# A linear-attention block and a multilayer perceptron on one core: a new order for the same instructions

## The chip, the core and the metric

The kernel runs on one core of a Trainium2 chip. The metric is the device time of one execution in microseconds (us); a kernel's time is the median of its runs. A core has a TensorE (matrix products; PE in the profile, its weight loads PEld), a VectorE (DVE), a ScalarE (ACT), a GpSimd (POOL) and a SyncE (SP), which here only issues transfers (DMAs). Each engine works through its own list of instructions in order and waits on semaphores for the others.

## The reference

Four batches of 768 tokens, eight heads of 48 elements. First a gated linear attention, then a block with layer norm and two matrices of 384 x 1536 and 1536 x 384:

```python
for t in range(S):
    state = alpha[:, :, t, :, None] * state + np.einsum('bhd,bhe->bhde', k[:, :, t], v[:, :, t])
    y[:, :, t] = np.einsum('bhd,bhde->bhe', q[:, :, t], state)
...
x = y.transpose(0, 2, 1, 3).reshape(B, S, H * D)
xn = (x - mu) / np.sqrt(var + 1e-06) * g_ln
out = x + np.maximum(xn @ w_ch1, 0.0) @ w_ch2
```

## The kernel before

The tokens are cut into six chunks (c = 0 to 5) of 128, and each chunk is worked on for four batches (b = 0 to 3). All matrix products are in float32, each of two TensorE instructions.

**Attention** (`attention`, L278): 24 generators, one for each chunk and batch. Each loads its inputs, takes the logarithm of the gates (L292), sums it along the tokens with a triangular matrix on TensorE (L298 in chunk 0, L303 later), takes exponentials (L306, L307), scales k and q on DVE (L309, L311), transposes them (L336), copies the transposes out of PSUM (L341, L343), forms the scores (L352 in chunk 0, L360 later), masks them on DVE (L367, L372), forms the update of the state (L388), adds it on DVE (L397, L401) and gates it on POOL (L403), forms the output (L414 in chunk 0, L426 for odd and L429 for even batches later), moves it out (L437 to L443), normalises it (L456 to L470), transposes it (L476) and scales it into xT (L479, L483). From chunk 1 on, the chunk is cut into halves of 64 tokens, so that L303, L360, L388, L426 and L429 are products on 64 or 48 rows that share the TensorE array.

**Weights** (`take_weights`, L229): the two matrices come as twelve pieces of 768 KB in 64-bit floats (six of the first matrix, six of the second), through three buffers `ws`. A piece is loaded (L205) and made 32-bit in three DVE instructions (L217, L219, L221), one on ACT (L223) and two on DVE (L225, L227); then the piece three further on is loaded into its buffer.

**Perceptron.** Chunk 0 uses the plain products: `hidden` (L506, with a ReLU on ACT, L509) and `project` (L518). Chunks 1 to 5 use fast matrix multiplications with fewer products: 15 products of combined blocks (`hidden_product`, L795) in two rounds for the first matrix, and 20 (`product`, L618) for the second. The combined blocks are made on DVE: of the first matrix once (`combine_first`, L744), of the second once (`combine_weights`, L578), of xT for each chunk (`combine_x`, L769), of the hidden values for each chunk (`combine_hidden`, L605). The results of the products are gathered by sums on DVE (L805 to L838, L628, L631) and POOL (L814 to L834, L634), the ReLUs of chunks 1 to 5 are on ACT (L846), and the outputs are sent by SP (L497).

**PSUM.** All TensorE results, of the attention and of the perceptron, share one pool of eight banks (`tag="bank", bufs=8`); an accumulator can be opened when a bank has been read out.

**The order.** Nothing is scheduled by the framework: each piece of work is a Python generator that yields after a few instructions, and the string `ORDER` (L25 to L46) says whose turn is next. The instructions of all engines, DMA issues too, are written down in the order of these turns. In this document turn n is the letter at place n of `ORDER`, counted from 0; there are 1566. The letters:

```python
turns = {"YZ"[h]: first_of_chunk_0(h) for h in range(2)}
turns |= {"PQ"[h]: second_of_chunk_0(h) for h in range(2)}
turns |= {chr(ord("a") + n): attention(n // B, n % B) for n in range(NCB * B)}
turns |= {chr(ord("A") + i): take_weights(i) for i in range(len(pieces))}
turns |= {"M": mlp(), "V": hidden_products(NCB - 1), "S": combine_first(), "W": combine_weights(), "R": relus(),
          "X": (x for c in range(1, NCB) for x in combine_x(c)),
          "N": (x for c in range(1, NCB) for x in combine_hidden(c)), "O": outputs()}
```

So a to x are the attentions, A to L the weight pieces, Y and Z the hidden layer of chunk 0 for batches 0, 1 and 2, 3, P and Q its projection, M the products of chunks 1 to 5 (without the first matrix of chunk 5, which is V), R the ReLUs, S, W, X and N the combinations, and O the loads of x for the output sums. M and V yield twice for each product: the TensorE instructions are one turn (four of L795 or eight of L618), the sums that read the accumulator the next.

Of the kernel before, what the change touches and what calls it, by code (L numbers as in the profile page):

```python
# [22 lines left out]


ORDER = (  # L25
    "acacababcdaacabdbaabdcacabbacbbababceccbaAcfcdbadaacecacfeafdedebdfbeadbaedeecge"
    "adbAacgAfedghbgeedfecfafgfcefdAgeddbbgfdfghffbebaigcjbibffhjBhcdcYhCfcgccehYfedh"
    "cfedeedhgdedYjAfidBfjiBZhjhZZfBYegfhgjhghCiZYBYiCYYhfhghhkggZilihjZjgiZCiDjYDZZZ"
    "ghZYEYjkeiYkiDiEijgljjjlghYCYhiYkhYFEZhiFigYEZigkikDYZZlkkeejlYlgjhFlZlmYkZgknlg"
    "jZSGkHmiknlSljlkiljkjlGiHlmlllZimFhmZYgYmmjZiYhmheeHmGlkfSnZlnZefSQnmfiGHZghkkeo"  # L30
    "IYmSkiISkJgjIjommmOmJPJnSnQgopPghlKPIKhKjiPOnLSnSfSXkmQLffQOLXWkimXPQSWmPPXpnOpW"
    "XmnnXSmXSQomWnnpnmSoXmQMlmlkXkWliMnnMoXXpjWSWSMjMMoMoMlSMnMMWMoMknMMpMMqMMMMMOPi"
    "npnMopMMrmOMjkpMpopopRqoMoirQkplppnqprRppqWMMWMMnMWMqlMRrMMMMkMqRMMMjkrqRMrMMpsk"
    "oMoMMqMMRRnqpMMRjMqMMoWqOqsnRpqlsoqqpMsNtRNpMMNMjNoMoMMMosRqMMMOkNooMqtNMNMMMtMo"
    "MRlNNsmkNMpqMMNtMMMNlMrMMNMMNqMtqMsrMMWNnrrqMMMNMMstnMXvMsMMvXXprXorrXXXrqMMMXXM"
    "MMMMMMMsXqMMOmvMMMMMMMuXMMMMMMmtRMmttMRrtMrMMttrstvMtqussvsqtMMMMqMrMMrvMMMrRMMM"
    "MRMtMnMRMMmssmrMrrpOtsORMuRMoRMsMMMMoRNMMNtMMNMpqMMMoRNMRNMNNMMNRNOMnNMMMrstMpMN"
    "toNMNMMMMMrMnuoOMsMuNMvxMMuMNrpMOMNovMMvMMvMpMMMXtXMxvvMsXvssXXsXtvMXMuMXuXMMMMM"
    "usMMMtwMMMMMMvMMvwuuuRuuXuuuLxvXOMMMMMMMMMMMwMwxMrMuMswMuMMMwMMsvRxRvMMsMMRwMMxM"
    "xMqwMxMMxMwRtMMMxwMMMMxRqruwtxRwxswxxwRxwuxwRMNvNwMRMNrvwNRMMMMMMtNwNNquNNRrsvst"  # L40
    "tMNMJxMOMMMNNMxMMMvMqMuwxxMNtMtMMMMxuwXMwMMNXMXMMNMvNMXXuMXMXMMxXMXwMMXwMMMvMwMM"
    "MxMMMMMMMXMMMMMOuMuMMRMMMMMMMMwMMMMMMMMMRMMvxMMRMRxwMMMROMuMRMvOwxMMRRMwMRxMNMOM"
    "uMvMMXRVNMMMXXMMRMXXXXMMNVNVXVVXMVNMMVVVMVRVNXVVVVVNRVVMNXVVMVRVMVMVNVNMNVVVMVMV"
    "VMRVRVMVVVMVMVONVMVMNMVMMMRVMNNVRVVVVMVVROVMMMVMNVRVVRVMVMVMNMVRKMOMMMRNNMNMMNMM"
    "MMMNVNMNMNVMMMMNRONMMMNMMNMMMNMMMMNMMMNMMMMMMM"
)  # L46


# [860 lines left out]
```

## Time and profile before

| | |
|---|---|
| median of three runs | 434.6 us |
| lowest and highest run | 433.5, 435.28 us |
| span of the profiled execution, first to last instruction | 431.0 us |
| median less this span | 3.6 us |
| mean granted TensorE clock | 0.999 |
| instructions | 11676 |
| moved by DMA | 45.53 MB |

The profile is one execution; its own time isn't given beside its span, so the 3.6 us are the part of a median run that lies around the span. Lines such as L618 are those of the kernel's source; "out<-in" names tiles, without their buffer numbers. "busy" is the time in which an engine ran an instruction, "idle before" the time that it stood still ahead of one, followed by what ended the wait. The chain of waits is followed back from the last instruction, at each step to what released it; its rows have a start, a length, and an engine with tile, line and number of instructions. Ends of matmuls are modelled, and some matmul records are missing, so counts in rows can be low.

### The profile page before, as it was taken

The page shows a single profiled execution, that of the slowest core. Times are in us where ns is not written, and L with a number is a line of the kernel's source. Part 1 is how long each engine was busy: PE and PEld are TensorE (multiplying, and loading weights), DVE is VectorE, ACT ScalarE, POOL GpSimd, SP SyncE. Part 2 cuts the span into 40 slices and gives each one's busy share as a digit, 9 for nine tenths or more (in the row PEclk, how much of TensorE's full clock was granted, in tenths as well). Part 3 has the DMA queues.
Part 4 walks back from the last instruction along what each step waited for, and adds up shares of the span by engine and source line. Part 5 has one row for each costly group of instructions (what it writes and reads, how often), then busy time and mean ns, then how long its engine had stood idle before and what let it go on. Part 6 is the DMA issues. An engine that isn't in the chain of part 4 may idle for free.

```text
span 431.0 us, 11676 instructions
## 1 busy us (share of the span) xinstructions
PE 425.7 (99%) x4760; PEld 378.2 (88%) x4760; DVE 333.2 (77%) x644; ACT 200.0 (46%) x519; POOL 152.7 (35%) x164
## 2 busy tenths in 40 slices
PE   8999999999999999999999999999999999999997
PEld 6788888866588889998889998889998899999996
DVE  4989899999998888866769756757686668948683
ACT  6597466774043882325385134384415562221100
POOL 1011031110205382252563243580153661647423
PEclk9999999999999999999999999999999999999999
DMA  8979968774117354031150141400014000011201
GB/s 287 288 208 272 308 151 257 203 247 142 38 56 212 107 148 141 29 105 45 52 151 23 49 120 38 94 2 22 2 56 146 2 1 2 0 39 37 75 18 55
DMA packets 55517, 45.53 MB, mean 106 GB/s; under 512 B 26748, under 2 KB 51580, under 8 KB 55464
## 3 DMA queue, kind: packets, MB, share of 16 engines
q1 hardware_dynamic: 54920, 44.63, 35.0%
q8 instruction: 37, 0.61, 0.6%
q10 hardware_dynamic: 544, 0.17, 0.2%
q14 instruction: 16, 0.13, 0.1%
HBM read 35.25 MB, written 9.53 MB: 104 GB/s over the span
## 4 chain that ended last, share of the span: by engine, by line
PE 94%; DVE 2%; DMA 1%; ACT 1%; SPq 0%; issue 0%; DVEq 0%
PE hps L795 30%; PE ops L618 30%; PE ops L518 7%; PE hps L506 6%; PE tps L336 4%; PE aps L360 3%; PE ups L388 2%; PE yps L426 2%; PE yps L429 2%; PE xps L476 2%; DMA ws<-in_moe_w_ch_dram 1%; PE lps L303 1%; PE aps L352 1%; PE lps L244 1%; PE lps L298 1%; PE yps L414 1%
## 5 line engine op out<-in xcount | busy, mean ns | idle before, releaser
L795 PE MATMUL hps<-sum,w 128*128 128x256 f32 x192 | 48.0, 381 | 0.0
L634 POOL TENSOR_TENSOR ob<-ob,u 128x192 f32<-128x192 f32 x40 | 27.0, 685 | 58.9 <-DVE ob L631 44.3
L618 PE MATMUL ops<-w,hT 128*128 128x192 f32 x224 | 40.7, 328 | 0.0
L795 PEld LDWEIGHTS hps<-sum,w 128*128 128x128 f32 x192 | 35.7, 190 | 4.7 <-ACT hT L825 0.2
L618 PEld LDWEIGHTS ops<-w,hT 128*128 128x128 f32 x224 | 36.9, 190 | 1.0 <-issue 0.6
L403 POOL TENSOR_TENSOR mid<-mid,gate 112x192 f32<-112x192 f32 x20 | 13.3, 668 | 68.7 <-DVE mid L401 19.7
L795 PE MATMUL hps<-xT,w 128*128 128x256 f32 x136 | 34.4, 380 | 0.0
L506 PE MATMUL hps<-xT,w 128*128 128x256 f32 x144 | 34.0, 384 | 0.1
L846 ACT ACTIVATE hT<-hT 128x512 f32<-128x512 f32 x48 | 28.8, 625 | 10.4 <-POOL hT L817 7.1
L518 PE MATMUL ops<-w,hT 128*128 128x384 f32 x96 | 32.8, 490 | 0.0
L628 DVE TENSOR_TENSOR ob<-ops,ob 128x192 f32<-128x192 f32 x50 | 17.6, 353 | 17.7 <-PE ops L618 9.4
L506 PEld LDWEIGHTS hps<-xT,w 128*128 128x128 f32 x144 | 26.3, 190 | 4.0 <-DVE xT L479 0.6
L618 PE MATMUL ops<-ws,sum 128*128 128x192 f32 x160 | 29.2, 327 | 0.0
L814 POOL TENSOR_TENSOR hT<-hT,u 128x512 f32<-128x512 f32 x8 | 10.4, 1305 | 53.0 <-DVE u L813 53.0
L795 PEld LDWEIGHTS hps<-xT,w 128*128 128x128 f32 x136 | 25.5, 190 | 3.2
L518 PEld LDWEIGHTS ops<-w,hT 128*128 128x128 f32 x96 | 17.6, 190 | 10.5
L618 PEld LDWEIGHTS ops<-ws,sum 128*128 128x128 f32 x160 | 26.4, 190 | 0.2
L336 PE MATMUL tps<-consts,qk 128*112 128x128 f32 x176 | 25.3, 275 | 0.2 <-DVE qk L311 0.2
L336 PEld LDWEIGHTS tps<-consts,qk 128*112 128x112 f32 x176 | 20.3, 134 | 4.3 <-DVE qk L311 0.8
L460 ACT ACTIVATE xn<-x,few 128x384 f32<-128x384 f32 x24 | 14.8, 615 | 18.7 <-DVE few L456 17.5
L618 PE MATMUL ops<-ws,hT 128*128 128x192 f32 x128 | 23.4, 327 | 0.0
L618 PE MATMUL ops<-more,sum 128*128 128x192 f32 x120 | 22.0, 327 | 0.0
(243 smaller groups left out, 1172.9 us busy)
## 6 DMA issues: line engine op xcount, KB each, us to landing
ws<-in_moe_w_ch_dram SPq DMA_DIRECT2D x12, 768.0 KB
vn<-in_v_dram SPq DMA_DIRECT2D x12, 384.0 KB
kept<-x SPq DMA_DIRECT2D x24, 192.0 KB
ob<-kept SPq DMA_DIRECT2D x24, 192.0 KB
out_dram<-ob SPq DMA_DIRECT2D x19, 192.0 KB
ra<-in_alpha_dram SPq DMA_DIRECT2D x14, 192.0 KB
rk<-in_k_dram SPq DMA_DIRECT2D x6, 384.0 KB
rq<-in_q_dram SPq DMA_DIRECT2D x6, 384.0 KB
```

The source lines that it names most:

```text
L336: nc.tensor.transpose(tps[:, p], qk_of(c, b)[:, i, p].rearrange("p a b -> p (a b)")[:, :R], ident)
L360: nc.tensor.matmul(aps[0][halves[i if cross else 1 - i], p, s], kT[rs, p, s], qT[rs, p, s], start=True, stop=True)
L403: nc.gpsimd.tensor_mul(new, new, by)
L460: act(out=xn, in_=x, func=AFT.Square, bias=mean, accum_out=dev)
L506: nc.tensor.matmul(hps, w1[:, j // 2, f, j % 2 * P:][:, :P], xT_of[0][:, f, bs], start=(f == 0), stop=(f == NF - 1))
L518: nc.tensor.matmul(ops_of[b], hT_of[c][:, j, b], w2[:, j], start=(j == 0), stop=(j == NJ - 1))
L618: nc.tensor.matmul(acc, lhs[:, j], rhs[:, j], start=(j == 0), stop=(j == NT - 1))
L628: nc.vector.tensor_add(x, acc, x)
L634: getattr(nc.gpsimd, f"tensor_{op}")(x, x, y)
L795: nc.tensor.matmul(acc[:, i], w, b, start=True, stop=True)
L814: add_late(c4, c4, u2)
L846: nc.scalar.activation(out=x, in_=x, func=AFT.Relu)
```

## The change

Turns 0 to 61 and the last seven stay. All others are put in a new sequence. Each letter occurs as often as before, so every generator issues the same instructions in its own order; the instructions, tiles, buffers and engines are the same, and the order between generators differs, on every engine and on SP.

```diff
 ORDER = (
-    "acacababcdaacabdbaabdcacabbacbbababceccbaAcfcdbadaacecacfeafdedebdfbeadbaedeecge"
-    "adbAacgAfedghbgeedfecfafgfcefdAgeddbbgfdfghffbebaigcjbibffhjBhcdcYhCfcgccehYfedh"
-    "cfedeedhgdedYjAfidBfjiBZhjhZZfBYegfhgjhghCiZYBYiCYYhfhghhkggZilihjZjgiZCiDjYDZZZ"
-    "ghZYEYjkeiYkiDiEijgljjjlghYCYhiYkhYFEZhiFigYEZigkikDYZZlkkeejlYlgjhFlZlmYkZgknlg"
-    "jZSGkHmiknlSljlkiljkjlGiHlmlllZimFhmZYgYmmjZiYhmheeHmGlkfSnZlnZefSQnmfiGHZghkkeo"
-    "IYmSkiISkJgjIjommmOmJPJnSnQgopPghlKPIKhKjiPOnLSnSfSXkmQLffQOLXWkimXPQSWmPPXpnOpW"
-    "XmnnXSmXSQomWnnpnmSoXmQMlmlkXkWliMnnMoXXpjWSWSMjMMoMoMlSMnMMWMoMknMMpMMqMMMMMOPi"
-    "npnMopMMrmOMjkpMpopopRqoMoirQkplppnqprRppqWMMWMMnMWMqlMRrMMMMkMqRMMMjkrqRMrMMpsk"
-    "oMoMMqMMRRnqpMMRjMqMMoWqOqsnRpqlsoqqpMsNtRNpMMNMjNoMoMMMosRqMMMOkNooMqtNMNMMMtMo"
-    "MRlNNsmkNMpqMMNtMMMNlMrMMNMMNqMtqMsrMMWNnrrqMMMNMMstnMXvMsMMvXXprXorrXXXrqMMMXXM"
-    "MMMMMMMsXqMMOmvMMMMMMMuXMMMMMMmtRMmttMRrtMrMMttrstvMtqussvsqtMMMMqMrMMrvMMMrRMMM"
-    "MRMtMnMRMMmssmrMrrpOtsORMuRMoRMsMMMMoRNMMNtMMNMpqMMMoRNMRNMNNMMNRNOMnNMMMrstMpMN"
-    "toNMNMMMMMrMnuoOMsMuNMvxMMuMNrpMOMNovMMvMMvMpMMMXtXMxvvMsXvssXXsXtvMXMuMXuXMMMMM"
-    "usMMMtwMMMMMMvMMvwuuuRuuXuuuLxvXOMMMMMMMMMMMwMwxMrMuMswMuMMMwMMsvRxRvMMsMMRwMMxM"
-    "xMqwMxMMxMwRtMMMxwMMMMxRqruwtxRwxswxxwRxwuxwRMNvNwMRMNrvwNRMMMMMMtNwNNquNNRrsvst"
-    "tMNMJxMOMMMNNMxMMMvMqMuwxxMNtMtMMMMxuwXMwMMNXMXMMNMvNMXXuMXMXMMxXMXwMMXwMMMvMwMM"
-    "MxMMMMMMMXMMMMMOuMuMMRMMMMMMMMwMMMMMMMMMRMMvxMMRMRxwMMMROMuMRMvOwxMMRRMwMRxMNMOM"
-    "uMvMMXRVNMMMXXMMRMXXXXMMNVNVXVVXMVNMMVVVMVRVNXVVVVVNRVVMNXVVMVRVMVMVNVNMNVVVMVMV"
-    "VMRVRVMVVVMVMVONVMVMNMVMMMRVMNNVRVVVVMVVROVMMMVMNVRVVRVMVMVMNMVRKMOMMMRNNMNMMNMM"
-    "MMMNVNMNMNVMMMMNRONMMMNMMNMMMNMMMMNMMMNMMMMMMM"
+    "acacababcdaacabdbaabdcacabbacbbababceccbaAcfcdbadaacecacfeafdeeeabfddaddbbbceeeA"
+    "caecdfeedcgadeehbbbbeegfgbgdhddgaAbaghffffgbdgAgehefhffgecfffBddccicdChjfcYehhhc"
+    "fhfcdieYdgggehghejhgjfhffdfYhjjjjidBZYBZeiZijZijAhghgiBghiiijBZCZZkCCYkiZiijlYij"
+    "lejjkYhgYkiZDYhZZhkDYYZggYkkkljkhfhgDCkiEilEYlgEFEYDlZZFlZhgliFYFjillYYYYZjHHlmk"
+    "lSklkjlGkYkYYGZZZZiZZZlnGiinmZHgmgglllmkmngYIQimYmjmmInjmQjlGikoIkmOIfheHlkkSjjo"
+    "hkghhiSiJnJmmmmmkSPoPknnJoPeLjSPKkQSeeenLjKnnQpOKnepOSnOlonSffpfnLmnWnmmSSPPSfmP"
+    "pghPfjhmmgpSXlmjXXkXXkXkinkQSXWXmnSQOXQQlXiMkiiiXWMWnMMMMSlMMMSSMMkpMMMMMMMoMMnr"
+    "oMMoMoWpkqpopMMMMOnqopoopoprmRRmpWpopnMpRpmMoqqnMWrqMMqWRRMMMMMMMWMpMMMMMMMOMqqq"
+    "lMMpMMjMjMMMqMpMMqnrrsjoRRRrostMtRqoqqqqoppnooWqpqWoNWNMqRRRMMNNqMMNNsMsslONNsNM"
+    "MMMMMMMMMMMMNpmmNMWNmMMqllpllooONMoMMMMMpNNttoMMtosumssMMNrMMrrrMMstMMMrXXXXXXXs"
+    "vqqqrvrrXXXMMMMMXrrMMMMMMMMMMMMMMnMnRpJnOqopOMMMMMMMMMMMMMMMMMMMMMMMMpMpRMMtMMRM"
+    "MOnMRttrnrurMssssttttsrrvvvrsrstttRtRMtMMtMRuuMtMRRNRtMRuNNNMMMMMRNNMNMMMruqNMMM"
+    "MMMMooMMMsssNNNqMqNvNvMvwvMxMMMMNMMMMvNNuuuusrsvuwsquuuuvuuuMussxxvsxvvtvtXvXXww"
+    "wXXwXXXXMMMMMMMMMMMMMMMMMXXxMMMMMMMMMMMMMMMMMMMMsvvOORtxtstRttOrMMMMMMMMMMMMMMMM"
+    "MMMMMMMxRxMMtxxwrwwwrMMMsxMRwxRwxwxxwwvRxxwuwRvqwRRRuuMwMNMMMMrOxRMRMNMstMxMwNNN"
+    "NNMxxxwwwwwxxNMNMuuNxMwwMNuuNMMMMMxMuMMMNMMMMqNrwXNNXvvvXvvMMuMMXXXXXOMMMMMMMMXM"
+    "MOMMMMXXMMMMMMMMMMMMMMMMMMMMMMMMMMMMMMMMMMMMMMMMMRMMMMMMMMMMRRRRMMMMMRuRRROOxMMw"
+    "RvNMNNNxRNRvNNNNMMMMMMMMMMMMMNNNXXXXXXXXXXXMMMMMMNVVMMMMVVVVVVVVVVVVVVMMNNVVKVVV"
+    "VVVVVVVVOVVVVVVVVMMVVVVVVVVVVVVVVVVVVVVNVVVRRRRRRRRRRRRMMMMMNNNNNONLMMMMONMMNNNN"
+    "MMMMMMMMMMMNNMOMMMMMMMMMMMMMNNMMMMMMNMMMMMMMMM"
 )
```

## The prediction

> **What bounds the kernel now.** I read the page first, then who waited for whom, then the chain of waits stretch by stretch.
>
> ```profile
> span 431.0 us, 11676 instructions
> ...
> PE 425.7 (99%) x4760; PEld 378.2 (88%) x4760; DVE 333.2 (77%) x644; ACT 200.0 (46%) x519; POOL 152.7 (35%) x164
> ...
> PE 94%; DVE 2%; DMA 1%; ACT 1%; SPq 0%; issue 0%; DVEq 0%
> ```
>
> TensorE is busy 425.7 of 431.0 us, and the chain that ended last is 94% its own work. Next, the waits that ended TensorE's idle time:
>
> ```profile
> PE lps L244 <- DVE more L241: 1.1, 1, 1.1
> PE aps L352 <- DVE kT L341: 0.8, 1, 0.8
> PE tps L336 <- DVE qk L311: 0.2, 1, 0.2
> ```
>
> Three waits, 2.1 us, on the warm-up (L244) and on chunk 0 (L352, and the first L336), which the 62 turns that stay issue. Matmul ends are modelled, so a busy TensorE can hide short pauses. I look for them in the chain, and one place shows work of others in it:
>
> ```profile
> 32.25 6.02 DMA ws<-in_moe_w_ch_dram
> ...
> 43.85 2.83 PE hps L506 x12
> ```
>
> Weight piece B landed 6.02 us after its issue, at 38.27, and the hidden product that reads it started 5.6 us later, when the conversion was done. Behind it the chain is nearly all TensorE. So the new order can win little from waits. What is left is what TensorE's own instructions cost, and a sequence changes that only through their neighbours.
>
> **Part 1: detours.** L303, L360, L388 (from chunk 1 on), L426 and L429 use a 64-row form of the array, all else after 32 us the 128-row form. The chain shows what going from one to the other and back costs:
>
> ```profile
> 107.73 2.58 PE ops L518 x8
> 110.31 0.60 PE ups L388 x25
> 110.91 7.94 PE ops L518 x24
> ...
> 126.71 0.43 PE ups L388 x22
> ```
>
> Eight L518 take 2.58 us behind their own kind. The 24 behind the detour should take 3 x 2.58 = 7.74 and took 7.94: 0.20 us to come back. Going in: the same update product costs 0.60 us as a stretch of its own and 0.43 at the end of an open one, 0.17 us. Together 0.37 us on top of the work. Writing out the matmuls of every turn in both lists gives 25 stretches of 64-row work before and 20 after: 0.37 x 5 = 1.85, **-1.9 us**. Bounds: -1.0 (entry costs nothing) and -2.4 (entry 0.28, if the records missing from x22 hid 0.1).
>
> **Part 2: paired L303.** An L303 turn alone can stand in the open; two of an even and an odd batch run beside each other:
>
> ```profile
> 31.79 0.88 PE L303 MATMUL lps<-la,consts 64*64 64x384 f32 x8
> ```
>
> ```profile
> 167.56 1.08 PE yps L429 x64
> ...
> 169.09 0.66 PE lps L303 x3
> ```
>
> One takes 0.66 us at the end of its stretch, a pair 0.88. Pairs with no other matmul between: two before (turns 52 and 56, 134 and 139), three after (52 and 56, 347 and 348, 669 and 672). One more pair saves 2 x 0.66 - 0.88 = 0.4. Others lie beside L360 work that covers some of them, so I take **-0.3**, bounds -0.4 and 0.
>
> **Part 3: weights A to F.** The pieces are issued in nearly the old order (B at turn 141, was 140; C at 149, was 147), so I let B land near 38.3 us as before, 5.6 us ahead of its use. Between B's first turn (195) and its first reader (Z, turn 222) TensorE has work at these prices:
>
> ```profile
> 71.82 1.30 PE hps L506 x6
> 73.12 0.44 PE tps L336 x4
> ```
>
> Two hidden products, three sets of transposes, two updates and a detour: 2 x 1.30 + 3 x 0.44 + 2 x 0.43 + 0.37 = 5.2 us. The wait stays about as it is: **0**, bounds -0.2 and +0.6 (5.6 against 5.2, and 0.2 for a longer SP queue).
>
> **Part 4: piece J, a wait that is added.** The product P at turn 426 reads J, and J's last conversion is turn 424; before they were turns 422 and 430, with another P between. What is queued behind P is all of TensorE. DVE's prices:
>
> ```profile
> L217 DVE TENSOR_SCALAR w<-ws x12: 545/552/561, 21.4 to 103.3; 128x768 int32<-128x768 int32 x12
> L219 DVE SCALAR_TENSOR_TENSOR w<-ws,w x12: 957/957/959, 22.0 to 103.9; 128x768 f32<-128x768 uint32 x12
> L221 DVE TENSOR_SCALAR ws<-ws x12: 561/564/796, 23.0 to 104.9; 128x768 int32<-128x768 int32 x12
> L225 DVE SCALAR_TENSOR_TENSOR ws<-ws x12: 944/958/1257, 27.6 to 108.3; 128x768 int32<-128x768 int32 x12
> L227 DVE SCALAR_TENSOR_TENSOR w<-w,ws x12: 957/959/1145, 28.6 to 109.4; 128x768 f32<-128x768 f32 x12
> ```
>
> From turn 384 to 424 DVE has I's end (0.958 + 0.959 = 1.92), J's start (0.552 + 0.957 + 0.564 = 2.07), J's end (1.92) and nine others (three L401, three L744, L311, L372, L456), at DVE's mean of 333.2 / 644 = 0.52 us: 4.7. Together 10.6 us; J's step on ACT lies beside the nine. TensorE has, before turn 426, 32 L360, two output products (L426, L429; 1.0 us each is the 1.08 above less an entry), L303, two P, L336 and the way back:
>
> ```profile
> 75.04 0.78 PE aps L360 x36
> ```
>
> 0.7 + 2 x 1.0 + 0.66 + 2 x 2.58 + 0.44 + 0.20 = 9.2 us. But a duration on DVE is more than its share of the queue:
>
> ```profile
> 387.93 0.68 DVE L813 TENSOR_TENSOR rq<-rk,hps 128x512 f32<-128x512 f32 x1
> 388.53 0.69 DVE L605 TENSOR_TENSOR sum<-hT,sum 128x512 f32<-128x512 f32 x1
> 389.13 1.76 DVE L605 TENSOR_TENSOR sum<-sum,hT 128x512 f32<-128x512 f32 x1
> ```
>
> 0.68 and 0.69 long, they start 0.60 apart: 0.08 of each lies beside the next. Over the 14 pairs of neighbours that is 1.1 us, and J is late by 10.6 - 1.1 - 9.2 = 0.3: **+0.3**, bounds 0 and 1.5 (no overlap).
>
> **Part 5: bunches on DVE.** The new list puts 12 L605 and 11 L769 between turns 1362 and 1402. Behind them wait the evictions that free the eight PSUM banks: the accumulator of turn 1388 is evicted at 1403, and turn 1418's (V) is the one that needs its bank.
>
> ```profile
> 322.69 21.58 PE hps L795 x100
> ...
> 409.69 18.21 PE ops L618 x112
> ```
>
> ```profile
> L605 DVE TENSOR_TENSOR sum<-hT x16: 676/683/1162, 162.6 to 374.5; 128x512 f32<-128x512 f32 x16
> L605 DVE TENSOR_TENSOR sum<-sum,sum x15: 681/684/1539, 174.2 to 423.4; 128x512 f32<-128x512 f32 x15
> L769 DVE TENSOR_TENSOR sum<-xT x12: 415/419/814, 107.3 to 322.5; 128x256 f32<-128x256 f32 x12
> ```
>
> ```profile
> L628 DVE TENSOR_TENSOR ob<-ops,ob 128x192 f32<-128x192 f32 x50 | 17.6, 353 | 17.7 <-PE ops L618 9.4 <-ACT u L678 3.2 <-ACT u L665 2.4
> ```
>
> A turn of L618 is eight instructions, 8 x 18.21 / 112 = 1.30 us; one of L795 four, 4 x 0.216 = 0.86. From turn 1362 to 1418 TensorE has 12 and 2 of them, 15.6 + 1.7 = 17.3 us. DVE has until 1403 12 x 0.683 + 11 x 0.419 + 10 evictions x 0.353 = 8.2 + 4.6 + 3.5 = 16.3 us. One microsecond is left: **0**, bounds 0 and +0.6 (if DVE is already 1.6 late when the bunch begins, as it was with J at the worst). A full DVE alone is no loss, as a stretch of before shows (behind the length: TensorE, weight loads, DVE, ACT, POOL):
>
> ```profile
> 230.00:240.00 10.00, 10.00 (x65) 9.98 (x64) 9.97 (x24) 4.46 (x12) 0.41 (x1) 1.00 0.00 1
> ```
>
> DVE was busy 9.97 of 10 us, and TensorE's 65 matmuls fill the stretch at L618's 0.163 us each: no room for a pause.
>
> **Sum:** -1.9 - 0.3 + 0 + 0.3 + 0 = -1.9 us on a span of 431.0, so 429.1. The median of the runs is 434.6; I take the 3.6 us around the span as they are: **432.7 us**. Half a per cent, about what a measurement of this kernel can tell from no change, is 2.2 us: the forecast lies just inside.
>
> **Rivals.**
> Faster, 431.8: the entry costs its upper bound (-2.4), the pair saves 0.4, J is hidden, no other wait comes in: -2.8. For it: the waits view shows that the old list, with DVE 77% busy, hid nearly all. Against it: two more DVE instructions in front of J lose 1 us again.
>
> Slower, 437.4: POOL slows DVE's bunch between turns 1362 and 1402, and V at 1418 waits for its bank. The L605 at 389.13 took 1.76 us instead of 0.68, and it stood beside a sum on POOL:
>
> ```profile
> 388.69 1.65 POOL L814 TENSOR_TENSOR qk<-qk,rq 128x512 f32<-128x512 f32 x1 [1.49 <-DVE rq L813]
> ```
>
> At 1.162 for each L605 (the longest of its row) the bunch takes 13.9 + 4.6 + 3.5 = 22.0 us against 17.3, late by 4.7: 432.7 + 4.7 = 437.4. The sign turns from 2.9 us of slowing on (1.0 of slack, 1.9 of gain). For it: seven POOL sums of chunk 4 stand in turns 1326 to 1345, so the last of them run beside the first L605. Against it: from turn 1346 to 1411 the list holds no POOL work. [...]
>
> Slower, 438.1: a transfer. If B took twice its 6.02 us behind the loads that stand on SP now, Z at turn 222 would start some 6 us late, of which part 3's bounds cover 0.6: 432.7 + 5.4. Against it: the order of issue up to C is nearly the old one.
>
> That the engines don't run the new list can be left out: each engine's stream is written in its order.
>
> **How the numbers follow.** Forecast 0.45, faster 0.35, DVE rival 0.14, transfer 0.06. The forecast's own range is 431.6 to 434.9 (the bounds of the parts, those of one side not all at once). The range that is to hold 8 in 10 goes below the faster rival by the 1.1 us that the lowest of the runs lies under their median, to 430.6, and up to 436.5, where the slower rivals come in by half. Faster by over 0.5%: the faster rival and a little of the forecast, 0.38. Slower by over 0.5%: 0.18, within it 0.44.
>
> **What would show it.** 20 stretches of 64-row work, each with 0.20 us more on the full-row matmuls behind it (part 1). The L303 of turns 669 and 672 in one piece under 0.9 us (part 2). A pause of TensorE ahead of the third P, ended by L227 (part 4). None ahead of V's third product, with the L605 of chunk 4 at 0.68 (part 5; 0.9 or more speaks for the rival). Waits of TensorE beyond 2 us after the first 12, or more than 2% of DMA in the chain, would make the forecast wrong.

## The result, and the profile after

The new list takes 432.62 us (median of 12 runs, 432.1 to 433.49), the old one beside it 434.76 (432.78 to 436.89): a ratio of 0.9951, 95% interval 0.9934 to 0.9969. That is 2.1 us less (1.3 to 2.9), where 432.7 was forecast. But the profiled execution of the new list has a span of 431.6 us, *longer* than the 431.0 of the old list's profile. What follows is about that contradiction.

The page of the new list (span, busy time by engine, chain by engine):

```profile
span 431.6 us, 11685 instructions
...
PE 423.8 (98%) x4760; PEld 378.5 (88%) x4760; DVE 333.0 (77%) x644; ACT 202.4 (47%) x519; POOL 153.1 (35%) x164
...
PE 96%; DMA 1%; SPq 0%; issue 0%; DVE 0%; ACT 0%; DVEq 0%
```

TensorE is busy 1.9 us less than the 425.7 of before, just the sum forecast, and more of the chain is its own. The busy time proves little by itself: in two later profiles of the old list (e12, e1) it is 426.1 and 426.7 us, in a second one of the new list (e2) 423.2. Who ended its idle time in the new list (line, releaser, us in total, times, longest):

```profile
PE aps L360 <- issue: 1.3, 1, 1.3
PE tps L336 <- DVE qk L311: 1.2, 1, 1.2
PE lps L244 <- DVE more L241: 1.1, 1, 1.1
PE lps L298 <- ACT la L292: 0.7, 1, 0.7
PE aps L352 <- ACT qT L343: 0.3, 1, 0.3
```

The last four stand in the first 12.4 us, before the turns that changed, and vary from run to run (the first L303 starts at 17.1 to 18.4 us in the profiles below, e8 left out). The first row is new: a pause of 1.3 us for which no semaphore answers. No transfer and no DVE instruction ends a wait after 12 us.

The chain of the new list at three places, for parts 1 and 2 (start, length, what):

```profile
26.46 0.48 PE lps L303 x2
...
27.53 0.79 PE lps L303 x4
...
83.83 0.66 PE lps L303 x8
...
86.42 2.58 PE ops L518 x8
...
96.06 5.36 PE ops L518 x16
...
101.86 7.74 PE ops L518 x24
...
114.03 0.45 PE ups L388 x24
114.47 2.78 PE ops L518 x8
...
162.66 0.70 PE lps L303 x6
```

Eight L518 take 2.58 us behind their own kind and 2.78 behind a 64-row stretch: the forecast 0.20. The L303 at 83.83 and 162.66 are the pairs of turns 347/348 and 669/672, in one piece each.

To compare lists without the start, I take the time from the start of the first L303 (its turn is in the part that stays) to the start of the last L618, and the part of it behind the last L518. Both are read from the first and last starts of these lines in each trace:

| run | 64-row stretches | first L303 to last L618, us | last L518 to last L618, us | median, us | ratio to the old list [95%] |
|---|---|---|---|---|---|
| old list, first profile | 25 | 410.3 | 304.3 | | |
| old list, e1 | 25 | 411.7 | 304.3 | 434.12 | 1.0005 [0.9987, 1.0023] |
| old list, e12 | 25 | 411.1 | 304.3 | 434.46 | 0.9996 [0.9972, 1.002] |
| new list | 20 | 409.9 | 299.9 | 432.62 | 0.9951 [0.9934, 0.9969] |
| new list, e2 | 20 | 409.5 | 299.9 | 432.19 | 0.9961 [0.994, 0.9982] |
| e3, first 500 turns new | 24 | 414.1 | 305.0 | 436.93 | 1.0076 [1.0053, 1.01] |
| e4, rest new | 21 | 410.5 | 300.8 | 434.41 | 1.0022 [0.9996, 1.0047] |
| e5, five detours back | 25 | 411.6 | 302.0 | 434.85 | 1.0015 [0.9997, 1.0032] |
| e6, twelve back | 32 | 412.9 | 302.0 | 435.85 | 1.0028 [1.0013, 1.0043] |
| e7, stretch broken | 21 | 408.7 | 299.9 | 431.45 | 0.9931 [0.9907, 0.9955] |
| e8, 56 small warm-up matmuls | 20 | 412.2 | 301.0 | 456.77 | 1.0514 [1.0489, 1.0539] |
| e9, two warm-up matmuls | 20 | 408.2 | 299.9 | 432.2 | 0.9942 [0.9921, 0.9964] |

(The times from the last L518 on can be compared only among lists with the same last 1000 turns, since the last L518 has other work behind it in the old list.)

### The profile page after: what moved, and what is told of

It reads as the page before. It is cut to its first block, busy times and chain, and to the rows that moved or that the text cites. A ratio compares the mean times of both kernels' runs of the same rounds, so it can differ in the third digit from the quotient of the medians.

```text
span 431.6 us, 11685 instructions
## 1 busy us (share of the span) xinstructions
PE 423.8 (98%) x4760; PEld 378.5 (88%) x4760; DVE 333.0 (77%) x644; ACT 202.4 (47%) x519; POOL 153.1 (35%) x164
## 4 chain that ended last, share of the span: by engine, by line
PE 96%; DMA 1%; SPq 0%; issue 0%; DVE 0%; ACT 0%; DVEq 0%
PE ops L618 30%; PE hps L795 30%; PE hps L506 7%; PE ops L518 7%; PE tps L336 5%; PE aps L360 4%; PE ups L388 3%; PE yps L426 2%; PE yps L429 2%; PE xps L476 2%; DMA rq<-in_q_dram 1%; PE lps L303 1%; PE aps L352 1%; PE yps L414 1%; SPq L137 0%
## 5 line engine op out<-in xcount | busy, mean ns | idle before, releaser
L634 POOL TENSOR_TENSOR ob<-ob,u 128x192 f32<-128x192 f32 x40 | 28.2, 714 | 82.9 <-DVE ob L631 61.8
L618 PE MATMUL ops<-w,hT 128*128 128x192 f32 x224 | 40.2, 327 | 0.0
L618 PEld LDWEIGHTS ops<-w,hT 128*128 128x128 f32 x224 | 36.7, 190 | 0.3
L846 ACT ACTIVATE hT<-hT 128x512 f32<-128x512 f32 x48 | 27.6, 628 | 13.6 <-DVE hT L838 4.5
L506 PE MATMUL hps<-xT,w 128*128 128x256 f32 x144 | 33.2, 383 | 0.0
L518 PE MATMUL ops<-w,hT 128*128 128x384 f32 x96 | 32.6, 489 | 0.0
L506 PEld LDWEIGHTS hps<-xT,w 128*128 128x128 f32 x144 | 26.6, 190 | 3.6 <-issue 0.2
L618 PE MATMUL ops<-ws,sum 128*128 128x192 f32 x160 | 28.8, 326 | 0.0
L628 DVE TENSOR_TENSOR ob<-ops,ob 128x192 f32<-128x192 f32 x50 | 17.1, 352 | 14.8 <-PE ops L618 4.5
L518 PEld LDWEIGHTS ops<-w,hT 128*128 128x128 f32 x96 | 17.7, 190 | 10.8
L618 PEld LDWEIGHTS ops<-ws,sum 128*128 128x128 f32 x160 | 26.3, 190 | 0.1
L336 PE MATMUL tps<-consts,qk 128*112 128x128 f32 x176 | 23.5, 274 | 1.2 <-DVE qk L311 1.2
L336 PEld LDWEIGHTS tps<-consts,qk 128*112 128x112 f32 x176 | 20.0, 134 | 4.1 <-DVE qk L311 1.8
L618 PE MATMUL ops<-ws,hT 128*128 128x192 f32 x128 | 23.4, 326 | 0.0
L343 ACT COPY qT<-tps 112x512 f32<-112x512 f32 x24 | 14.1, 586 | 18.6 <-PE tps L336 18.4
```

The source lines that it names most:

```text
L336: nc.tensor.transpose(tps[:, p], qk_of(c, b)[:, i, p].rearrange("p a b -> p (a b)")[:, :R], ident)
L343: nc.scalar.copy(out=qT, in_=tv)
L506: nc.tensor.matmul(hps, w1[:, j // 2, f, j % 2 * P:][:, :P], xT_of[0][:, f, bs], start=(f == 0), stop=(f == NF - 1))
L518: nc.tensor.matmul(ops_of[b], hT_of[c][:, j, b], w2[:, j], start=(j == 0), stop=(j == NJ - 1))
L618: nc.tensor.matmul(acc, lhs[:, j], rhs[:, j], start=(j == 0), stop=(j == NT - 1))
L628: nc.vector.tensor_add(x, acc, x)
```

## The experiments

The theory on record: five detours fewer, 0.37 us each. The first rival: early transfers that the old list waits for in most runs, though not in the profile that the forecast was made from. A third cause came up with the pause.

**Both lists again, unchanged: e1, e2, and e12 last of all.** No edit.

> The kernel before, once more, for a second profile and for the spread of its runs. Theory A (the gain is TensorE's own: five detours fewer, 1.9 us, the same in every execution): ratio 1.000; the second profile has its TensorE waits in the first 12 us only, as the first one had, and TensorE's time beyond its own instructions after turn 62 is within 0.5 us of the first profile's. Theory B (the gain is in waits on transfers: the old list waits in most executions, and the first profile, a 431.0 us span under a median of 434.7, was a lucky one): a profile near the median has 1 to 3 us of TensorE waits in the first 125 us that the first one had not.

> The changed kernel, once more, for a second profile. Its first profile holds a pause of 1.3 us among L360 at 74.4 us, ended by nothing that the profile shows, and is the slowest of its 12 runs (433.49, median 432.62). Theory A: ratio 0.995 to 0.996; if the pause belongs to the sequence it is there again at the same instructions, and if it was of that one execution it is gone and the span is 430.5 or less. Theory B: the same ratio, and no wait on transfers after turn 62.

> The old list, unchanged, for a third profile of it. The first profile's span of 431.0 stands for a run of 432.9 (1.9 to 2.1 us lie around every span so far), the second's of 432.8 for one of 434.9. If a run of the old list near its median (434.1 to 434.8) carries waits on early loads that the first profile lacked: TensorE's way from the first L303 to the last L618 takes 411 us or more with a longer L303 at 32 us or a wait ahead of L506, when the profiled run is above 434, and about 410.3 when it is near 433. If the spread of its runs comes from the start or from outside the span: 410.3 to 410.5 whatever the run's time, and the difference ahead of the first L303 or around the span.

The profiled runs took 434.92 us (e1, span 432.8), 431.95 (e2, span 430.0) and 434.13 (e12, span 432.1): 1.9 to 2.1 us lie around a span. So the old list's first profile was a run of about 433.0, near its fastest, and the new list's a run of 433.49, its slowest of twelve. That settles the contradiction, and shows that the 3.6 us of the forecast were not all around the span: 1.6 of them are time that a typical run of the old list spends inside. Where, the waits of TensorE in e1 say,

```profile
PE tps L336 <- DVE qk L311: 1.1, 1, 1.1
PE lps L244 <- DVE more L241: 1.1, 1, 1.1
PE hps L506 <- DVE w L227: 0.5, 1, 0.5
```

and its row for L303 (window 31.4 to 33.5 us: idle time of its engines until, us, times), its chain from 27 us on:

```profile
  ACT la L292: 0.9, 2
```

```profile
27.78 3.67 DMA ra<-in_alpha_dram
...
31.47 0.53 ACT la L292
...
34.05 6.17 DMA ws<-in_moe_w_ch_dram
```

The load of chunk 2's alpha was issued at 27.78 us (26.09 in the first profile), and the pair of L303 waited 0.9 us for its logarithm. Piece B followed at 34.05 (32.25), and the hidden product that reads it waited 0.5 us for L227. In e12 the second wait is there again, with the same 0.5 us, and of the first only 0.2. In both profiles of the new list there is neither. There B's last L227 ends 0.5 us before the first L506 that reads it starts (46.51 + 0.96 = 47.47 against 47.94; in e2 46.20 against 46.70). What e1 expected of theory B is met (1.4 us of early waits), and so is e12's first case: over 411 us on the way in runs above 434. In e2 the pause is there again at the same L360, 1.1 us long.

**One half of the new list alone: e3 and e4.**

```diff
-ORDER = old
+ORDER = new[:500] + what is left over, in the old sequence   (e3)
+ORDER = old[:500] + what is left over, in the new sequence   (e4)
```

> The first 500 turns of the new list (all loads of weights but none of the later inputs' are in them), then what is left of the old list in its old order: 24 stretches of 64-row work, old 25, new 20. Theory A: one detour fewer, -0.4 us, ratio 0.999. Theory B: nearly the whole gain, -1.5 to -2.2 us, ratio 0.995 to 0.9965.

> The first 500 turns of the old list, then what is left of the new list in its order: 21 stretches of 64-row work. Theory A: four detours fewer, -1.5 us, ratio 0.9965. Theory B: none of the gain, ratio 0.999 to 1.001.

Both are misses: neither half gains, though e4 has 21 stretches, four fewer than the old list. The seams bring waits of their own. In e3 the generators reach turn 500 at other places than the old list had them, and TensorE waits for sums of chunk 1 that come late:

```profile
PE hps L795 <- DVE hT L805: 0.7, 1, 0.7
PE lps L303 <- DVE hT L827: 0.5, 1, 0.5
PE hps L795 <- DVE u L813: 0.3, 1, 0.3
```

In e4 the seam joins two stretches into one of 260 matmuls, and a pause like the new list's stands there, with a wait for xn just behind the seam:

```profile
PE yps L426 <- issue: 1.2, 1, 1.2
...
PE xps L476 <- ACT xn L470: 0.8, 1, 0.8
```

So these two decide nothing on the detours. In e3 the three waits and its pause (1.1 us) are 2.6 of the 3.8 us by which its way is longer than that of the old list's first profile; the rest was not traced. In e4, whose profile is its fastest run (433.1 us), the way less the pause and the wait is 408.5 us, 1.8 below the old list's first profile: about four detours, worked out and not shown. The pause of e3 is the new list's, at the same L360: it comes with the early half.

**Detours put back: e5 and e6.** The last turn of a stretch goes behind the full-row turn that follows; one of the five places of e5, and the one of e6's early seven that matters for its output:

```diff
-    turns 601 to 603 of the new list:  p (L388)  m (ACT)  M (L795)
+                                       m (ACT)  M (L795)  p (L388)
...
-    turns 281 to 284:  i (L388)  l (L309)  E (ACT)  Y (L506)
+                       l (L309)  E (ACT)  Y (L506)  i (L388)
```

In e6 that last move lets the update product of batch 0 in chunk 2 read a buffer into which batch 3's k has gone; the instructions and their shapes are the same, but e6 does not compute the reference's output. Its times serve for the detours alone.

> The new list with five detours put back: at five places behind turn 500 the last turn of a 64-row stretch goes behind the first full-row turn that followed, so that 25 stretches stand where 20 stood, and the first 500 turns stay the new ones. If the detours carry the gain (0.37 us each): 1.9 us slower than the new list, 434.2 to 434.5, a ratio of 0.999 to 1.000 to the kernel before. If the gain comes from the early transfers (25 to 50 us): nothing is lost, ratio 0.995 to 0.996.

> As the run with five detours back, with seven more of them between turns 100 and 506: 32 stretches. If a detour costs 0.37 us: 4.4 us slower than the new list, 436.7 to 437.0, ratio 1.005 to 1.006, and a slope of 0.37 us for each stretch from 20 over 25 to 32. If the early transfers carry the gain: the new list's time, up to 0.5 us more, ratio 0.995 to 0.997.

The late five are the same in both. First and last start of the last L518 and L618 of e2, e5 and e6:

```profile
L518 PE MATMUL ops<-w,hT x96: 486/486/590, 84.8 to 126.7; 128*128 128x384 f32 x96
...
L618 PE MATMUL ops<-w,at x24: 326/326/326, 400.7 to 426.6; 128*128 128x192 f32 x24
```

```profile
L518 PE MATMUL ops<-w,hT x96: 486/486/590, 85.6 to 127.5; 128*128 128x384 f32 x96
...
L618 PE MATMUL ops<-w,at x24: 326/326/326, 403.7 to 429.5; 128*128 128x192 f32 x24
```

```profile
L518 PE MATMUL ops<-w,hT x96: 486/486/590, 85.7 to 128.5; 128*128 128x384 f32 x96
...
L618 PE MATMUL ops<-w,at x24: 326/326/326, 404.7 to 430.5; 128*128 128x192 f32 x24
```

426.6 - 126.7 = 299.9 us without them, 302.0 and 302.0 with: 2.1 us for five, **0.43 each**. The early seven of e6, against e9, which like it has no pause: 110.96 - 108.29 = 2.67 us from the first L303 to the last L518, 0.38 each. The detour is shown, a little dearer than forecast. e5 as a whole is 1.4 to 3.0 us over the new list's two spans (433.0 against 431.6 and 430.0), as expected of the detours; e6 came out below its 436.7 since it has no pause, on which more below.

**The pause: e7, e8, e9.** The chain of the new list at the pause:

```profile
72.89 0.55 PE ups L388 x23
...
73.49 0.94 PE aps L360 x55
74.43 1.32 issue
75.75 0.33 PE aps L360 x3
```

TensorE stops three matmuls before the end of a dense stretch. A count shows what is special there. The windows view gives TensorE's matmuls and weight loads up to it (behind the stretch: length, TensorE, weight loads, each with its count):

```profile
0.00:75.60 75.60, 71.18 (x1229) 60.57 (x1229) 59.88 (x114) 48.45 (x120) 9.92 (x17) 1.00 0.84 249
```

With the 39 semaphore and drain instructions that stand on its queue up to there, 2 x 1229 + 39 = 2497 = 9 x 256 + 193. In e4 the pause came elsewhere:

```profile
0.00:123.70 123.70, 120.54 (x1869) 95.48 (x1869) 107.87 (x200) 73.23 (x184) 16.55 (x26) 1.00 0.73 213
```

2 x 1869 + 39 = 3777 = 14 x 256 + 193: 1280 instructions, 5 x 256, beyond the first place. And just ahead of the pause the new list's DMA view (72.9 to 74.1 us) has a packet of the instruction queue, 16 KB:

```profile
q8 instruction: 1, 0.02, 6.1%
```

Three edits: a product put into the stretch (e7; from turn 312 on), and two that shift the count of instructions but leave the order alone.

```diff
-    YZjHHlmklSklkjlGkYkYYGZ
+    YZjHHlmklYSkYlkjlGkkYGZ          (e7)
...
-    for _ in range(8):
-        nc.tensor.matmul(idle[:, :P], zero, zero, start=True, stop=True)
+    for _ in range(56):
+        nc.tensor.matmul(idle[:, :8], zero, zero[:, :8], start=True, stop=True)   (e8)
+    for _ in range(2):
+        nc.tensor.matmul(idle[:, :P], zero, zero, start=True, stop=True)          (e9)
```

> The new list with two turns of piece Y's letter (an eviction and a hidden product of six L506) moved seven to eight places earlier, into the stretch of 32 L388 and 64 L360 at 73 us in which TensorE paused for 1.1 to 1.3 us. If TensorE outran its refill of instructions there: the product gives it 1.3 us of slow work, the pause is gone, one detour of 0.37 more: 0.7 to 0.9 us below the new list, ratio 0.993 to 0.994. If the pause is a wait for data of the L360: it stays, and the time is 0.4 above the new list.

> The new list with 56 small warm-up matmuls (8 columns) in place of 8 (128 columns), which puts 192 more instructions ahead of all else: a block of 256 instructions then ends behind the stretch at 73 us, among L506. If the refill of instructions makes the pause: it is gone from L360, and the time is 1.1 to 1.3 us below the new list, ratio 0.992 to 0.993, unless another long 64-row stretch (120 to 123 us, 143 to 146 us) gets one. If the pause is a wait for data: it stays at the same L360, and the ratio is 0.995 to 0.996. The start may cost up to 1 us either way.

> The new list with 2 warm-up matmuls (L244) in place of 8: 24 instructions fewer ahead of all else, so that the block of 256 that ended among the last L360 of the stretch at 73 us ends 20 instructions behind that stretch, among L506 of 0.2 us each. If the refill of instructions makes the pause: gone, 1.1 to 1.3 us below the new list, 431.0 to 431.5, ratio 0.992 to 0.9935. If the pause belongs to the order of the turns (a data wait): it stays at the same L360, ratio 0.995 to 0.9965. TensorE waits for data at the start either way, so six warm-up matmuls fewer should win nothing there; if they do, the spans gain it before the first L506.

e7, the chain at the same place: no pause, one detour more, 408.7 us on the way, 0.8 to 1.2 below the new list. Its median of 431.45 us is the lowest of all (ratio 0.9931 [0.9907, 0.9955] to the old list), but the interval overlaps the new list's, so the profile shows the gain and the times only agree with it:

```profile
73.36 0.53 PE aps L360 x26
73.89 1.49 PE hps L506 x6
75.39 0.84 PE aps L360 x30
```

e9, the same order as the new list, 24 instructions fewer in front:

```profile
73.51 1.00 PE aps L360 x58
74.51 4.51 PE hps L506 x20
```

No pause either, and the way is 408.2 us, 1.3 to 1.7 shorter than the new list's. Its median of 432.2 lies above the 431.0 to 431.5 expected and does not show the whole of that: this profile's start is 0.2 to 1.3 us later than the new list's two (first L303 at 18.4 us), within what the start varies in these runs, so on its time e9 is inconclusive and on its profile clear.

e8 as a time is a miss (456.77 us, ratio 1.0514 [1.0489, 1.0539]): the 56 small matmuls hold TensorE for 24 us at the start. For the question it answers: at the L360 of the new list's pause there is none, and other stretches have four. The waits of TensorE in e8:

```profile
PE ups L388 <- issue: 1.6, 2, 1.3
...
PE aps L360 <- issue: 0.9, 1, 0.9
PE yps L426 <- issue: 0.3, 1, 0.3
```

The longest stands at 2 x 1990 + 53 = 4033 = 15 x 256 + 193, as the windows view and the chain there show; that is 1536 instructions, 6 x 256, beyond the place in the new list. For the others an estimate, worked out from the new list's trace with e8's 192 instructions put ahead: 193 beyond 5, 24 and 27 x 256 lie an L360, an L388 and an L426, the lines of the three shorter waits (0.9, 0.3 and 0.3 us).

```profile
0.00:144.40 144.40, 139.96 (x1990) 115.84 (x1990) 102.60 (x190) 75.78 (x190) 15.02 (x26) 1.00 0.63 184
```

```profile
142.87 0.31 PE ups L388 x15
143.18 1.35 issue
144.53 0.38 PE ups L388 x8
```

So the pause belongs to a place in the stream of instructions, not to the data of the L360: shown by e8 and e9, which have the new list's order and another count, and by e7, in which six L506 (1.49 us) stand ahead of the last L360. What the traces have beside it is the instruction queue: 37 packets of 16 KB for 9620 instructions of TensorE in the new list and 38 for 9812 in e8, one for each 260 and 258, and in the new list TensorE goes on at 75.75 us, 2.8 us after a packet began (72.94). The old list and e6 pass instruction 2497 inside or at the end of a dense stretch too, without a pause. There the packet of the instruction queue came before the stretch began: at 69.8 us against 73.5 in the old list, between 71.0 and 73.8 in e6, whose stretch stands in its chain from 73.9 on; in the new list it came at 72.9, when the stretch had begun (72.8). These figures agree with a TensorE that outran its instructions; no view shows what it had left, so that is the author's reading. Why the packet starts later there was not tried.

**More transfers: e10 (old list) and e11 (new list).**

```diff
+                if n == "a" and c == 2 and m == 0:
+                    more_of = dram.tile([2, P, H * D], FP32, name="more_of", tag="more_of")
+                    nc.sync.dma_start(more_of, k[0:2, 0:P].rearrange("b t h d -> b t (h d)"))
                 t = raw.tile([P, 2, 2, NP, D], FP32, name=f"r{n}", tag="in", bufs=6)
```

> The old list with one more transfer: a copy of 384 KB within DRAM, issued on SP ahead of the load of chunk 2's first pair of alpha (the ra that L292 reads at 30 to 32 us). If the old list's typical run loses to early row loads: the L303 at 32 us stands 0.6 us behind the end of its L292, so a transfer that lands 1.3 to 2.6 us later (384 KB at 290 to 150 GB/s) costs 0.7 to 2.0 us, ratio 1.002 to 1.005, with a TensorE wait ended by L292 or a longer L303 at 32 us. If these loads are hidden in the old list: no change, ratio 1.000.

> The new list with the same copy at the same place. Here the two L303 stand 2.1 and 2.8 us behind the end of their L292, and piece B is 0.5 us ahead of its product. If the new list's gain is in part a larger margin for row loads: 0 to 0.7 us, ratio 0.995 to 0.998, and the gap between the two lists grows by about 1 us. If not: it loses as much as the old list does with the copy.

442.43 us (ratio 1.018 [1.0154, 1.0207]) and 440.53 (1.0131 [1.0106, 1.0155]): both lose about 8 us, several times what was expected, and the gap of 1.9 us between the lists stays. Not all of it is the wait: TensorE's granted clock stands at 5 tenths in e10's page from 33.2 to 44.2 us (at 7 and 8 in e11's from 32.9 to 54.9), where the pages of the two lists without the copy have 9 throughout, and behind the wait six L506 (L509 in that kernel) took 2.86 us in e10, from 41.52 us on, where 1.30 was the price. The load behind the copy landed 10.89 us after its issue in e10, against 3.67 in e1, and each list waits some 7 us, at different lines (lines from 134 on stand three higher in these two kernels; e10's chain and wait, then e11's wait):

```profile
27.97 10.89 DMA ra<-in_alpha_dram
```

```profile
PE lps L306 <- ACT la L295: 7.3, 1, 7.3
```

```profile
PE xps L479 <- DVE xn L469: 6.7, 1, 6.7
```

Whether the new list has a larger margin these two can't tell: a delay of 7 us is far over either margin, and what the new list saves at L303 it loses a little later. The early waits of the old list are seen in two of three profiles, and are not there in the two of the new; that they make up the rest of the difference is worked out, not shown by a run of its own.

## Why the prediction was right

The number was right, and the mechanism half of it: the detours were counted and priced nearly right, and that the rest cancelled is luck. By the prediction's own steps:

- **What bounds the kernel.** That "the new order can win little from waits" held for the profile it was read from and fails for a typical run: 0.5 us for piece B in e1 and e12, 0.9 for a row load in e1.
- **Part 1, detours.** Right: 20 stretches, 0.20 us on the way back (2.78 against 2.58), and e5 and e6 give 0.38 to 0.43 for a whole detour where 0.37 was taken. Five fewer: 1.9 to 2.1 us.
- **Part 2, pairs.** The pairs came, in 0.66 and 0.70 us, under the 0.9 that was named. But two L303 of chunk 1 that stand at 26.46 and 27.53 us in the new list take 0.48 and 0.79 us of TensorE's way by themselves. The prediction counted the pairs and not the ones that come into the open: about 0 for the 0.3, an estimate, since no run moves the L303 alone.
- **Part 3, pieces A to F.** 0 was right for the new list. The term was measured from the wrong end: the old list's B is late in a typical run, not the new one's.
- **Part 4, piece J.** No wait: the L518 from 96.06 to 112.95 us stand without a hole between them and the L336 and L476 among them. 0 for +0.3.
- **Part 5 and its rival.** 0, as forecast. The bunch's L605 took their plain length, and no wait stands ahead of V. Two later ones, at 375.2 and 376.9 us, took 1.78 and 1.07 us, with no wait of TensorE behind them. (New list, 340 to 395 us; shortest, median, longest in ns, first and last start of four of the bunch:)

```profile
L605 DVE TENSOR_TENSOR sum<-hT x4: 683/684/685, 354.0 to 361.8; 128x512 f32<-128x512 f32 x4
```

- **What no part had: the pause.** +1.1 to 1.3 us in a stretch that was made dense, for which nothing in the old profile stood.
- **The sum.** The step that failed is "I take the 3.6 us around the span as they are". Only 1.9 to 2.1 are; the rest is waits of a typical run. On the way of the profiled old list the new one wins 0.4 to 0.8 us (410.3 to 409.9 and 409.5): 1.9 to 2.1 from the detours, less 1.1 to 1.3 for the pause, and a tenth or two either way from the L303. Against the two typical profiles of the old list it is 1.2 to 2.2. Two things that were missed, the pause and the waits, are about equally large and of opposite sign.

The version to keep is e7: the new list with the dense stretch at 73 us broken by one hidden product.

## What to carry to other kernels

Before a forecast is made against one profiled span, compare that run's own time with the median: here the profile of a fast run lacked 1.4 us of early waits that a run near the median had (e1). Where the work goes in and out of a tiled form of TensorE, count the changes of form, and price one from two like rows: here 0.37 us, where runs gave 0.38 and 0.43. Look at what merging such stretches does: here TensorE paused for 1.05 and 1.32 us in a stretch of 96 very short matmuls, and with one product of slow matmuls in its middle the way was 0.8 to 1.2 us shorter (e7).

## What the hardware did that was not expected

- **TensorE paused at places that lie multiples of 256 instructions apart in its stream.** Seven pauses of 1.0 to 1.35 us (the new list, e2 to e5, e8, e11) stand in stretches of 64-row matmuls, where 55 L360 pass in 0.94 us. The three whose place is worked out above stand at instructions 2497, 3777 and 4033, 193 beyond 9, 14 and 15 x 256. Shorter ones, for which no semaphore answers either, are three of 0.3 to 0.9 us in e8 and one of 0.8 in e10. The instruction queue moved one packet of 16 KB for each 258 to 260 instructions of TensorE. That TensorE had no instructions left in the pauses is the author's reading of these figures and was not shown.
- **The warm-up matmuls cost nearly the same with 8 columns as with 128.** In e8 those of 128 x 8 took 24.1 / 112 = 0.215 us each, with 128 columns 3.8 / 16 = 0.24; the weight loads alone are busy for 24.0 and 3.5 us of it (e8, then the new list; busy time and mean ns behind the bar):

```profile
L244 PE MATMUL lps<-more 128*128 128x8 f32 x112 | 24.1, 361 | 1.1 <-DVE more L241 1.1
```

```profile
L244 PE MATMUL lps<-more 128*128 128x128 f32 x16 | 3.8, 431 | 1.1 <-DVE more L241 1.1
```

- **With a copy of 384 KB within DRAM issued ahead of it on SP, a load landed 7 us later after its issue** (10.89 us in e10 against 3.67 in e1), where 1.3 to 2.6 were expected from the rate of other transfers (about 290 and 150 GB/s, in slices of the old list's page that have 287 and 151). e10's page has six packets of 8 KB or more that the old list's has not; 384 KB in six would be 64 KB each, an estimate. The load was issued at 27.97 us and landed at 38.86.
